# Attention quads from the sixth on: another order of VectorE's work, a Newton step moved to GpSimd, output tiles joined, weight pieces moved

## The chip, the cores and the metric

The kernel runs on one core of a Trainium2 chip. A core has five engines that each take their own queue of instructions in order: TensorE (matrix products, PE in the profile, with its weight loads as PEld), VectorE (DVE), ScalarE (ACT), GpSimd (POOL) and SyncE (SP, which here only issues DMA transfers). Engines wait for each other through semaphores. The metric is the device time of one execution in microseconds; the time before is the median of three runs, 825.98 us (824.99 to 826.01).

## The reference

An attention block with normalised q and k feeds a block with a SoLU activation. Shapes: 8 batches, 12 heads, 448 positions, head size 64; 3584 tokens, 768 features, 1024 hidden columns. All in fp32.

```python
q_n = q / sqrt(mean(q*q, -1) + 1e-6) * g_q        # k_n likewise
scores = q_n @ k_n.T / sqrt(64)
attn = exp(scores - max) / (sum(exp(scores - max)) + 1e-9)
x = (attn @ v) laid out as tokens x (heads * 64)  # 3584 x 768
h = x @ w_in                                      # 768 x 1024
solu = h * softmax(h)
ln = (solu - mean) / sqrt(var + 1e-6) * g_ln
out = ln @ w_out                                  # 1024 x 768
```

The weights w_in and w_out come as 64-bit floats and are turned into fp32 in the kernel.

## The kernel before

`fast_path` has three stages: attention (0 to 332.7 us of the profile), the product with w_in and the activation (to about 585 us), and the product with w_out (to the end). The order of the work in each engine's queue is the order in which the Python code emits it, by hand; `later(x, f)` puts f off until x further units of TensorE work have been emitted.

**Attention.** Two heads of one batch are a pair; there are 48. Two pairs are a quad; the loop over `m` runs over 24 quads, and in quad m the pairs are `a = 2m` and `b = 2m + 1`. One quad's work on TensorE: `scores(a, 0..2)` (keys against queries, 128 of the 448 keys in each), `scores_last` (the last 64 keys of both pairs in one tile), `scores(b, 0..2)`, then `values_last` and `values` for both pairs (exponentials times v, into PSUM tiles `o`), then `sums` (exponentials times a matrix of ones, which gives the softmax's denominators). ScalarE takes the exponential of each score tile (L802) into `E`. There is no subtraction of the maximum: q and k are normalised, so the scores are bounded.

To save TensorE work in `sums`, VectorE adds tiles first. `add(n)` makes `es` from E of key blocks 0 and 1 (L839). In the last two quads (`on_vector`, L833) `add_more` adds block 2 as well (L844). In all other quads block 2 is a term of its own in `sums` (L884): five terms instead of three, each of four products.

`inverse(m)` reads the sums from PSUM (a transpose on VectorE, L895, then a reciprocal, L896), and GpSimd copies 32x14 pieces of `rc` across partitions (L903, four copies). `divide(m)`, one unit later, spreads `rc` with a transpose (L910) and multiplies the tile `o` by it (L911), for each of the two pairs. `store_x` sends the result `xo` to DRAM on SyncE's queue.

**Normalisation of q and k for the next quads.** `load(n)` issues eight DMAs of 56 KB for one pair into a tile `qk` (five buffers). `squares` (ScalarE, L656), `row_sums` (VectorE, L664), `fold_sums` (GpSimd, four copies L674 and an addition L675), `rsqrt_seed` (ScalarE, logarithm and exponential, L694 and L695), `rsqrt_step` (a Newton step of four small VectorE instructions, L701 to L704), `normalise` (GpSimd, L713, 128x896, 1.70 us), `qk_transpose` (VectorE, L723) and `gain` (ScalarE, L727) make `qkT` for the scores. In quads 4 to 22 of before, seed, step and both `normalise` stand at the head of a quad, the transposes near its middle, and the squares, row sums and fold for the quad after it at its end.

**w_in under the attention.** Twelve pieces of w_in (512 KB each) are loaded (`load_next`), converted in two steps on ScalarE (L535, L536) and two on VectorE (`join`, L541, L542), and combined on GpSimd (`combine_in`, L563, 1.28 us), since the two later products use a seven-multiplication scheme that needs differences of blocks. `steps_at` and `joins_at` say in which quad. In most quads `load_v`, `store_x`, the loads of the pairs of quad m + 3 and a piece of w_in follow each other on SyncE's queue.

**The first product.** `in_parts` runs over 14 groups of two token tiles; the products use PSUM banks A, B, C, D. After a tile's last product, `done` emits `ff_max` and then `ff_exp`, `ff_mult`, `ff_moments`, `ff_norm` (ScalarE, L1077) and `ff_spread` (a VectorE transpose and four DMAs), each put off by so many units. The last of these, for the last group, come among the first products with w_out, where ScalarE must copy partial results out of PSUM (L1206) and copy operands (L1149, L1151, L1153).

Of the kernel before, what the change touches and what calls it, by code (L numbers as in the profile page):

```python
# [9 lines left out]
FP32 = mybir.dt.float32  # L10
# [356 lines left out]
def fast_path(  # L367
# [329 lines left out]
    def rsqrt_step(d):  # L697
# [5 lines left out]
        nc.vector.tensor_tensor(x, x, y, OP.mult)  # L703
        nc.vector.scalar_tensor_tensor(y, x, 1.5, y, OP.add, OP.mult)  # L704

    def normalise(n, e=nc.gpsimd):
        d = st[n]
        if ("one", n) in norms:
            y = norms["one", n]["y"]
        else:  # L710
            y = norms[n // 2]["y"][:, n % 2 * 2 * NB : (n % 2 + 1) * 2 * NB]
        d["qkn"] = work.tile([P, 2 * NB, 32], FP32, tag="qkn", name="qkn", bufs=2)
        e.tensor_tensor(  # L713
            d["qkn"],
            d["qk"].rearrange("p s b d -> p (s b) d"),
            y.rearrange("p b -> p b ()").to_broadcast([P, 2 * NB, 32]),
            OP.mult,
        )
# [41 lines left out]
    def warm_up():  # L760

        w = work.tile([P, 2, S], FP32, tag="r", name="warm", bufs=1)[:, 0]
        nc.vector.memset(w, 0.0)
        o = ps_t.tile([P, S], FP32, tag="o", name="pt", bufs=2)
        for _ in range(5):
            nc.tensor.matmul(o, w[:, 0:P], w, start=True, stop=True)

# [5 lines left out]

    def transpose_rows(n, s):
        d = st[n]
        d["pt", s] = ps_t.tile([P, S], FP32, tag="o", name="pt", bufs=2)
# [53 lines left out]

    def on_vector(m):  # L833
        return m >= NQ - 2

    def add(n):
        d = st[n]
# [2 lines left out]

    def add_more(n):
        d = st[n]
        if on_vector(n // 2):
# [26 lines left out]
    def sums(m):  # L870


        d = quads[m]
        sm = d["sm"] = ps_t.tile([P, S // 2], FP32, tag="t", name="sm")
        terms = [(2, d["E", NJ])]
        for key in ("es",) if on_vector(m) else (2, "es"):
            for i in range(2):
                n = st[2 * m + i]
                terms.append((i, n["E", 2] if key == 2 else n["es"]))
        for x, (w, e) in enumerate(terms):  # L880
            for h in range(2):
                for t in range(2):
                    g = 32 * (2 * h + t)
                    nc.tensor.matmul(  # L884
                        sm[g : g + 32, :], ones[:, w], e[:, h, t * S // 2 : (t + 1) * S // 2],
                        start=(x == 0), stop=(x == len(terms) - 1),
                    )
# [15 lines left out]
                nc.gpsimd.tensor_copy(rc[o : o + 32, :, t], rc[a : a + 32, :, t])  # L903

    def divide(m):
        xo = quads[m]["xo"] = work.tile([P, 2, S], FP32, tag="xo", name="xo", bufs=1)
        for i in range(2):
            n = 2 * m + i
            r = work.tile([P, NB, 32], FP32, tag="r", name="r", bufs=1)
            nc.vector.transpose(r, quads[m]["rc"][:, i].rearrange("p t b -> p (t b) ()").to_broadcast([P, NB, 32]))  # L910
            nc.vector.tensor_tensor(xo[:, i], st[n]["o"], r.rearrange("d b i -> d (b i)"), OP.mult)  # L911
            del st[n]

    def store_x(m):
        b, hp = divmod(2 * m, NP)
# [52 lines left out]
    def products(g, done):  # L968
# [5 lines left out]
        def mul(bank, a, i, begin=True):  # L974
            a11, a12, a21, a22 = gs[g, "A"]
            sm = gs[g, "s"]
            a = {"a11": a11, "a12": a12, "s3": a21, "a22": a22, "s1": sm[:, 0], "s2": sm[:, 1], "s4": sm[:, 2]}[a]
            if begin:
                tag = "t" if bank in "AC" or bank == "B" and g == NG - 1 else "o"
                k[bank] = ps_t.tile([P, 512], FP32, tag=tag, name=bank, bufs=3 if tag == "t" else 2)[:, 0:n]  # L980
# [373 lines left out]
    with tc.manual_schedule():  # L1354
# [19 lines left out]
        for m in range(NQ):  # L1374
# [7 lines left out]
            next1 = m + 1 < NQ  # L1382
            next2 = m + 2 < NQ
            next3 = m + 3 < NQ
            if m == 0:
                unit(lambda: scores(a, 0))
                normalise_rows(1, 0)
# [326 lines left out]
```

## Time and profile before

| | us |
|---|---|
| median of three runs | 825.98 |
| the profiled execution | 827.41 |
| its span | 825.1 |
| attention, to the first product with w_in | 332.7 |
| quad 6 to quad 23, starts of the scores | 96.66 to 320.53 |
| TensorE busy | 802.1 |
| VectorE busy | 617.7 |
| ScalarE busy | 474.6 |
| GpSimd busy | 468.5 |

A line of the profile's groups gives source line, engine, operation, tiles (out<-in), shape and count, busy time and mean ns of one, and then the idle time in front with what ended it. A line of a timeline gives start and length in us, engine, line, operation, tiles, shape, count, and in brackets the idle time before it and its releaser. A line of stretches gives the stretch, its length, the busy time of each engine with the number of instructions, the granted TensorE clock (1.00 is full), the share of the DMA engines and GB/s.

### The profile page before, as it was taken

Reading aid. Unit: us, or ns where it says so; the run is one execution under the profiler, and the core shown is the slowest. Engines: PE = TensorE matmul, PEld = TensorE weight load, DVE = VectorE, ACT = ScalarE, POOL = GpSimd, SP = SyncE. Lnnn points to the kernel's source line nnn. Section 1 sums busy time; section 2 is a strip of 40 time slices with the busy share of each in tenths; the row PEclk is TensorE's granted clock in tenths of the full one; section 3 lists DMA queues with packets and bytes.
Section 4 is the critical chain, followed back from the end, with each engine's and each line's share of the span. In section 5 each row is a group of like instructions: output and inputs, shape, how many; then the busy total and the mean of one; then the engine's idle time right before and its main releaser. Section 6 shows DMA issues by size and latency. Waiting matters only on the chain.

```text
span 825.1 us, 14999 instructions
## 1 busy us (share of the span) xinstructions
PE 802.1 (97%) x5030; PEld 469.7 (57%) x5030; DVE 617.7 (75%) x1217; ACT 474.6 (58%) x785; POOL 468.5 (57%) x635
## 2 busy tenths in 40 slices
PE   8989999999999999999999999999799999999996
PEld 4333444333344443444444444444499999999996
DVE  6867889787888888378878766677776866866945
ACT  6676778676877777366666644444424464464420
POOL 1334545555555647333346467767387777877761
PEclk9999999999999999999999999999989999999999
DMA  7778677877777664235665335552547466475312
GB/s 132 146 140 195 145 177 162 186 150 173 156 176 169 134 158 120 84 104 133 180 163 152 92 97 133 135 143 67 153 128 244 141 219 213 137 248 195 131 58 82
DMA packets 272546, 122.74 MB, mean 149 GB/s; under 512 B 190540, under 2 KB 257612, under 8 KB 272460
## 3 DMA queue, kind: packets, MB, share of 16 engines
q1 hardware_dynamic: 257276, 111.79, 52.9%
q10 hardware_dynamic: 15184, 9.90, 4.4%
q8 instruction: 42, 0.69, 0.4%
q14 instruction: 44, 0.36, 0.1%
HBM read 84.94 MB, written 36.70 MB: 147 GB/s over the span
## 4 chain that ended last, share of the span: by engine, by line
PE 72%; SPq 6%; DVE 5%; DMA 4%; POOL 2%; issue 2%; ACT 2%; DVEq 0%; ACTq 0%; POOLq 0%
PE A L1194 15%; PE A L982 11%; PE B L1194 8%; PE o L865 7%; PE s L812 7%; PE B L982 7%; SPq L634 5%; PE C L982 4%; PE D L982 4%; PE C L1194 4%; PE sm L884 3%; DMA v<-in_v_dram 1%; PE s L825 1%; PE o L854 1%; DMA qk<-in_k_dram 1%
## 5 line engine op out<-in xcount | busy, mean ns | idle before, releaser
L802 ACT ACTIVATE E<-s 128x896 f32<-128x896 f32 x168 | 139.0, 935 | 14.3 <-PE s L812 14.1
L812 PE MATMUL s<-qkT 64*64 64x448 f32 x1152 | 121.3, 548 | 1.5 <-ACT E L802 0.9
L865 PE MATMUL o<-E,v 128*64 128x448 f32 x576 | 113.5, 543 | 0.0
L674 POOL COPY ss<-part 32x56 f32<-32x56 f32 x88 | 42.1, 478 | 99.2 <-DVE part L664 96.5
L713 POOL TENSOR_TENSOR qkn<-qk,ny 128x896 f32<-128x896 f32 x46 | 77.1, 1697 | 28.4 <-DMA qk<-in_k_dram 12.0
L1071 POOL TENSOR_TENSOR he<-he,mhalf 128x1 f32<-128x1 f32 x28 | 28.1, 1005 | 108.7 <-DVE he L1070 108.2
L812 PEld LDWEIGHTS s<-qkT 64*64 64x64 f32 x1152 | 47.3, 163 | 61.3 <-ACT E L802 31.6
L1194 PE MATMUL A<-w_out,sums 128*128 128x192 f32 x392 | 80.7, 329 | 1.1 <-ACT q L1206 0.7
L865 PEld LDWEIGHTS o<-E,v 128*64 128x64 f32 x576 | 39.2, 137 | 72.7 <-issue 64.0
L1194 PE MATMUL B<-w_out,sums 128*128 128x192 f32 x392 | 80.4, 328 | 0.0
L982 PE MATMUL B<-w_in,xsum 128*128 128x512 f32 x168 | 76.7, 593 | 0.6 <-POOL he L1071 0.6
L982 PE MATMUL A<-w_in,xg 128*128 128x512 f32 x168 | 74.7, 593 | 0.7 <-ACT u L989 0.7
L1053 ACT ACTIVATE u<-h,hmax 128x1024 f32<-128x1024 f32 x28 | 32.1, 1148 | 63.6 <-DVE hmax L1047 63.6
L1194 PEld LDWEIGHTS A<-w_out,sums 128*128 128x128 f32 x392 | 66.7, 191 | 2.2 <-issue 1.0
L1194 PEld LDWEIGHTS B<-w_out,sums 128*128 128x128 f32 x392 | 67.0, 192 | 0.1
L664 DVE TENSOR_REDUCE part<-sq 128x28 f32<-128x896 f32 x46 | 48.7, 1079 | 10.4 <-ACT sq L656 8.5
L982 PEld LDWEIGHTS B<-w_in,xsum 128*128 128x128 f32 x168 | 31.8, 190 | 41.1 <-issue 38.0
L982 PEld LDWEIGHTS A<-w_in,xg 128*128 128x128 f32 x168 | 31.8, 190 | 41.0 <-issue 39.1
L723 DVE STREAM_TRANSPOSE qkT<-qkn 128x896 f32<-128x896 f32 x46 | 49.0, 1093 | 6.6 <-POOL qkn L713 6.6
L839 DVE TENSOR_TENSOR es<-E 128x896 f32<-128x896 f32 x48 | 53.3, 1112 | 0.5 <-ACT E L802 0.5
L656 ACT ACTIVATE sq<-qk 128x896 f32<-128x896 f32 x46 | 43.5, 986 | 9.9 <-DMA qk<-in_k_dram 6.0
L1194 PE MATMUL A<-w_out,s 128*128 128x192 f32 x224 | 45.5, 326 | 0.0
(151 smaller groups left out, 1625.0 us busy)
## 6 DMA issues: line engine op xcount, KB each, us to landing
ur<-ud SPq DMA_DIRECT2D x60, 256.0 KB, 4.6
ud<-ub SPq DMA_DIRECT2D x112, 128.0 KB, 2.3
xd<-xo SPq DMA_DIRECT2D x24, 448.0 KB, 4.1
qk<-in_q_dram SPq DMA_DIRECT2D x184, 56.0 KB, 2.5
qk<-in_k_dram SPq DMA_DIRECT2D x184, 56.0 KB, 2.4
v<-in_v_dram SPq DMA_DIRECT2D x24, 384.0 KB, 4.2
out_dram<-P SPq DMA_DIRECT2D x19, 384.0 KB, 4.0
raw<-in_moe_w_in_dram SPq DMA_DIRECT2D x12, 512.0 KB, 5.1
```

What stands on the lines that cost most here:

```text
L634: nc.sync.dma_start(d["qk"][g * 32 : g * 32 + 32, s], src[b, h0 + g // 2].rearrange("(b t) (x d) -> x t b d", t=32, x=2)[g % 2],)
L656: nc.scalar.activation(d["sq"], d["qk"].rearrange("p s b d -> p (s b) d"), AF.Square)
L664: nc.vector.tensor_reduce(norms[m]["part"][:, i], st[n]["sq"], AX, OP.add)
L674: e.tensor_copy(ss[g * 32 : g * 32 + 32], part[o * 32 : o * 32 + 32])
L713: e.tensor_tensor(d["qkn"], d["qk"].rearrange("p s b d -> p (s b) d"), y.rearrange("p b -> p b ()").to_broadcast([P, 2 * NB, 32]), OP.mult,)
L723: nc.vector.transpose(d["qkT"].rearrange("p s t -> p (s t)"), d["qkn"].rearrange("p b d -> p (b d)"))
L802: nc.scalar.activation(d["E", kc], s[:, :, 0:S], AF.Exp)
L812: nc.tensor.matmul(s[c : c + D, h, 0:S], d["qkT"][hh, 1, keys], d["qkT"][hh, 0, :], start=True, stop=True,)
L839: nc.vector.tensor_tensor(d["es"], d["E", 0], d["E", 1], OP.add)
L865: nc.tensor.matmul(d["o"][h * D : (h + 1) * D, :], quads[n // 2]["v"][:, n % 2 * 2 + h, kc], d["E", kc][:, h], start=False, stop=(kc == NJ ...
L982: nc.tensor.matmul(k[bank], a[:, c], w_in[i][:, c], start=begin and c == 0, stop=c == HD - 1, skip_group_check=not begin,)
L1194: nc.tensor.matmul(k[bank], a[:, c].rearrange("p a i -> p (a i)"), w_out[:, area, i, c], start=begin and c == 0, stop=c == KC - 1, skip_gr ...
```

## The change

From quad 6 (`SETTLED`) on, a new branch of the loop emits the quad's work in another order:

- `load(a + 6)` comes before the first scores, ahead of `store_x`, and `load(b + 6)` behind it; `qk` has six buffers instead of five.
- `add_more` runs on VectorE for pair a of every quad from 6 on, and for both pairs from quad 21 on. The terms of `sums` follow that: four, then three.
- The seed stands behind `scores_last`; the Newton step is `rsqrt_step_apart`, five GpSimd instructions; both `normalise` follow it.
- The transposes of the next pairs stand behind `add(b)`; the row sums of pair a for the quad after the next at the quad's end, those of pair b at the head of the next quad, behind `inverse`, with `fold_sums`.
- The step `join` of a w_in piece stands between `add_more(a)` and `add(b)`.
- `steps_at` is 4 to 15, one piece in each quad; `joins_at` is one combination in each quad from 9 to 20.

In all quads, the two `o` tiles of a quad are one PSUM tile of two banks, and `divide` is one transpose and one product over both pairs. Banks B and D of the first product share that tile. The warm-up's and the first rows' tiles follow. For the last two groups of the first product the delays of the five steps are given one by one; those of the last group are longer.

```diff
-        d["qk"] = loads.tile([P, 2, NB, 32], FP32, tag="qk", name="qk", bufs=5)
+        d["qk"] = loads.tile([P, 2, NB, 32], FP32, tag="qk", name="qk", bufs=6)
...
+    def rsqrt_step_apart(d):
+
+        y, ss = d["y"], d["ss"]
+        p, w = ss.shape
+        x = small.tile([P, 4 * NB], FP32, tag="nx", name="nx", bufs=2)[0:p, 0:w]
+        nc.gpsimd.tensor_scalar(x, ss, -0.5 / D, -0.5e-6, OP.mult, OP.add)
+        nc.gpsimd.tensor_tensor(x, x, y, OP.mult)
+        nc.gpsimd.tensor_tensor(x, x, y, OP.mult)
+        nc.gpsimd.tensor_scalar(x, x, 1.5, 1.0, OP.add, OP.mult)
+        nc.gpsimd.tensor_tensor(y, x, y, OP.mult)
...
-    def on_vector(m):
-        return m >= NQ - 2
+    def on_vector(n):
+        m, i = divmod(n, 2)
+        return m >= NQ - 3 or m >= SETTLED and i == 0
...
     def values_last(m):
 
         d = quads[m]
+        o = d["o"] = ps_t.tile([P, 2, 512], FP32, tag="o", name="o", bufs=1)
         for i in range(2):
-            o = st[2 * m + i]["o"] = ps_t.tile([P, S], FP32, tag="o", name="o", bufs=2)
+            st[2 * m + i]["o"] = o[:, i, 0:S]
...
     def divide(m):
-        xo = quads[m]["xo"] = work.tile([P, 2, S], FP32, tag="xo", name="xo", bufs=1)
+        d = quads[m]
+        xo = d["xo"] = work.tile([P, 2, S], FP32, tag="xo", name="xo", bufs=1)
+        r = work.tile([P, 2 * NB, 32], FP32, tag="r", name="r", bufs=1)
+        nc.vector.transpose(
+            r, d["rc"].rearrange("p i t b -> p (i t b) ()").to_broadcast([P, 2 * NB, 32])
+        )
+        nc.vector.tensor_tensor(
+            xo, d["o"][:, :, 0:S], r.rearrange("d (i b) x -> d i (b x)", i=2), OP.mult
+        )
...
-            spread = {NG - 2: 7 - 2 * i, NG - 1: 8 - i}.get(g, 7)
-            for x, f in zip((1, 2, 3, 5, spread), (ff_exp, ff_mult, ff_moments, ff_norm, ff_spread)):
+            waits = {
+                (NG - 2, 1): (1, 2, 3, 5, 5), (NG - 1, 1): (1, 2, 3.25, 6.75, 7), (NG - 1, 0): (2.25, 3.75, 4.75, 7.5, 8)
+            }.get((g, i), (1, 2, 3, 5, 7))
+            for x, f in zip(waits, (ff_exp, ff_mult, ff_moments, ff_norm, ff_spread)):
...
-    steps_at = (4, 5, 6, 7, 8, 9, 10, 12, 14, 16, 18, 20)
-    joins_at = {9: (0,), 11: (1,), 13: (2,), 14: (3,), 15: (4,), 17: (5,), 19: (6,), 21: (7,), 22: (8, 9), 23: (10, 11)}
+    steps_at = tuple(range(4, 16))
+    joins_at = {9 + x: (x,) for x in range(12)}
+    SETTLED = 6
...
+            if m >= SETTLED:
+                for x in joins_at.get(m, ()):
+                    combine_in(x)
+                if next1:
+                    load_v(m + 1)
+                    if m > SETTLED:
+                        row_sums(b + 2)
+                        fold_sums(m + 1)
+                if next3:
+                    load(a + 6)
+                unit(lambda: scores(a, 0))
+                store_x(m - 1)
+                if next3:
+                    load(b + 6)
+                if m - 1 in sets:
+                    load_next()
+                unit(lambda: scores(a, 1))
+                unit(lambda: scores(a, 2))
+                unit(lambda: scores_last(m))
+                add(a)
+                if next1:
+                    rsqrt_seed(norms[m + 1])
+                    rsqrt_step_apart(norms[m + 1])
+                    normalise(a + 2)
+                    normalise(b + 2)
+                unit(lambda: scores(b, 0))
+                add_more(a)
+                step(m - 1)
+                unit(lambda: scores(b, 1))
+                add(b)
+                if next1:
+                    qk_transpose(a + 2)
+                unit(lambda: scores(b, 2))
+                add_more(b)
+                if next2:
+                    squares(a + 4)
+                if next1:
+                    gain(a + 2)
+                    qk_transpose(b + 2)
+                if next2:
+                    squares(b + 4)
+                if next1:
+                    gain(b + 2)
+                if next2:
+                    row_sums(a + 4)
+                begin(m)
+                unit(outputs)
+                unit(lambda: values(b))
...
+                unit(lambda: sums(m))
+                inverse(m)
+                if next1:
+                    later(1, lambda m=m: divide(m))
...
+                continue
```

More of the change, by code (lines that the diff above doesn't have):

```diff
@@ L763, in warm_up @@
         nc.vector.memset(w, 0.0)
-        o = ps_t.tile([P, S], FP32, tag="o", name="pt", bufs=2)
+        o = ps_t.tile([P, S], FP32, tag="t", name="pt")
         for _ in range(5):
@@ L775, in transpose_rows @@
         d = st[n]
-        d["pt", s] = ps_t.tile([P, S], FP32, tag="o", name="pt", bufs=2)
+        if s == 0:
+            d["pt"] = ps_t.tile([P, 2, 512], FP32, tag="t" if n else "o", name="pt", bufs=3 if n else 1)
+        d["pt", s] = d["pt"][:, s, 0:S]
         for j in range(4):
@@ L842, in add_more @@
         d = st[n]
-        if on_vector(n // 2):
+        if on_vector(n):
             nc.vector.tensor_tensor(d["es"], d["es"], d["E", 2], OP.add)
@@ L875, in sums @@
         terms = [(2, d["E", NJ])]
-        for key in ("es",) if on_vector(m) else (2, "es"):
+        for key in (2, "es"):
             for i in range(2):
-                n = st[2 * m + i]
-                terms.append((i, n["E", 2] if key == 2 else n["es"]))
+                n = 2 * m + i
+                if key == "es":
+                    terms.append((i, st[n]["es"]))
+                elif not on_vector(n):
+                    terms.append((i, st[n]["E", 2]))
         for x, (w, e) in enumerate(terms):
@@ L905, in divide @@
     def divide(m):
-        xo = quads[m]["xo"] = work.tile([P, 2, S], FP32, tag="xo", name="xo", bufs=1)
-        for i in range(2):
[L908 to L912, printed above, removed]
+        d = quads[m]
[7 more added lines that the diff above has]
+        )
+        for i in range(2):
+            del st[2 * m + i]
     def store_x(m):
@@ L978, in mul @@
             if begin:
-                tag = "t" if bank in "AC" or bank == "B" and g == NG - 1 else "o"
-                k[bank] = ps_t.tile([P, 512], FP32, tag=tag, name=bank, bufs=3 if tag == "t" else 2)[:, 0:n]
+                if bank in "AC" or bank == "B" and g == NG - 1:
+                    k[bank] = ps_t.tile([P, 512], FP32, tag="t", name=bank, bufs=3)[:, 0:n]
+                else:
+                    if "BD" not in k:
+                        k["BD"] = ps_t.tile([P, 2, 512], FP32, tag="o", name="BD", bufs=1)
+                    k[bank] = k["BD"][:, "BD".index(bank), 0:n]
             for c in range(HD):
@@ L1384, in fast_path @@
             next3 = m + 3 < NQ
+            if m >= SETTLED:
[46 more added lines that the diff above has]
+                unit(lambda: values(b))
+                if m == NQ - 1:
+                    block_sums(0, 0)
+                    block_sums(0, 1)
+                    load_x(1)
+                unit(lambda: sums(m))
+                inverse(m)
+                if next1:
+                    later(1, lambda m=m: divide(m))
+                if m == NQ - 2:
+                    load_x(0)
+                    sizes(0)
+                continue
             if m == 0:
```

## The prediction

> **What bounds the kernel now.** I read the page, then the stretches, the waits, and the timelines of single engines. The page gives a span of 825.1 us, 827.41 us for the profiled execution; the three runs have a median of 825.98 us. I work in differences and add them to the median.
>
> ```profile
> PE 802.1 (97%) x5030; PEld 469.7 (57%) x5030; DVE 617.7 (75%) x1217; ACT 474.6 (58%) x785; POOL 468.5 (57%) x635
> PE 72%; SPq 6%; DVE 5%; DMA 4%; POOL 2%; issue 2%; ACT 2%; DVEq 0%; ACTq 0%; POOLq 0%
> ```
>
> TensorE is the bound on average, but SyncE's queue holds 6% of the chain. Quad 17 and quad 13, by stretch (length, then PE, PEld, DVE, ACT, POOL busy):
>
> ```profile
> 251.50:264.40 12.90, 12.90 (x130) 5.44 (x128) 11.39 (x19) 9.14 (x14) 6.87 (x11) 1.00 0.73 160
> 199.90:212.80 12.90, 10.84 (x116) 4.22 (x118) 10.98 (x18) 9.68 (x14) 8.12 (x12) 1.00 0.75 159
> ```
>
> The first is a full quad of matmuls, 12.90 us. In the second TensorE loses 2.06 us. There SyncE is late: the square of q and k waits 3.3 us for its DMA, the sums on VectorE follow, and TensorE waits 1.5 us for `es`. SyncE issues the v load of quad 7 at 99.53 and of quad 22 at 300.28: 13.38 us a quad over 15 quads, nearly back to back, while its waits for engines there come to some 5 us. So the loads nearly pace quads 6 to 20. By the starts of L812, quad 6 begins at 96.66 and quad 23 at 320.53: 223.87 us for 17 quads, 13.17 each.
>
> Now VectorE against GpSimd. The sum `es` (L839), the fold's copies (L674), min/median/max in ns, and two pieces of timeline:
>
> ```profile
> L839 DVE TENSOR_TENSOR es<-E x48: 1046/1080/2161, 14.6 to 326.6; 128x896 f32<-128x896 f32 x48
> L674 POOL COPY ss<-part x88: 219/227/952, 29.3 to 307.7; 32x56 f32<-32x56 f32 x88
> 22.89 1.70 POOL L713 TENSOR_TENSOR qkn<-qk,ny 128x896 f32<-128x896 f32 x1 [2.16 <-DVE ny L704]
> 23.76 1.78 DVE L839 TENSOR_TENSOR es<-E 128x896 f32<-128x896 f32 x1
> ```
>
> The addition at 23.76 ends 0.95 us after GpSimd's product: it waited for it. A 0.22 us copy takes 0.95 us when an addition is under way, and ends just behind it. One excludes the other. Transposes, reductions and the products with PSUM next to L713 stretch neither side. Quads of before keep the additions away from the long products.
>
> Last, the start of the second product:
>
> ```profile
> 595.61 1.24 ACT L1077 ACTIVATE u<-u,shift,he 128x1024 f32<-128x1024 f32 x1 [4.19 <-POOL shift L1073]
> 597.63 1.65 PE L1194 MATMUL A<-w_out,a 128*128 128x192 f32 x4 [3.83 <-ACT u L1206]
> ```
>
> ScalarE's queue stands behind L1077, TensorE waits 3.83 us, and then four matmuls take 1.5 us instead of 0.81: the granted clock is half until 602.9.
>
> **What the Trainium skill says.** "GPSIMD Engine Reference", Specifications: GpSimd shares its SBUF interfaces with VectorE, and contends with VectorE instructions that have two SBUF inputs. The trace agrees (1.08 to 2.16 us for L839). "TensorE: Matmul & The Clock Gate", Part 1: an idle window of about 3.4 us halves the clock. The 3.83 us wait agrees.
>
> **The change, part by part.** *Ones products.* A term is eight records of L884; the group takes 2.03 us with five terms and 1.27 with three, so 0.38 us a term. Quads 6 to 20 lose one, quad 21 two: 17 x 0.38 = 6.5 us of TensorE. A quad would be 12.52 us.
>
> *Third additions.* One more L844 in those quads, 1.08 us alone, up to 1.89 against GpSimd. VectorE gives back Newton (0.13 + 0.24 + 0.22 + 0.22 = 0.81) and in `divide` four instructions become two: 2 x 644 + 2 x 624 = 2.54 becomes 1.09 (as L723, 896 wide) + 1.09 (624 plus 448 columns at the slope of L839 against L1208, 1.08 - 0.35 over 704) = 2.18. It is about even, with 11.4 us busy of 12.9 in a quad with a join.
>
> *Newton on GpSimd.* Five 128x56 instructions. The nearest row is L675, 302 ns, and 0.08 us of gap behind its producer. The bounds are 0.2 us (the copies) and 0.45 with gap; I take 0.38, 1.9 us.
>
> *The new order, where it costs.* `row_sums(b+2)` goes behind `inverse`, and `fold_sums`, seed, Newton and both `normalise` all fall into the same quad, ahead of `qk_transpose(b+2)` and `row_sums(a+4)`, which stand before the next `inverse` on VectorE. That closes a loop. Quads 9 to 16 (join and combine), t from the start of `inverse`:
> - VectorE: inverse 0.42 + 0.33; row sums end at 1.8. GpSimd: four rc copies (0.88) end at 1.83, combine (1.28) at 3.15, four fold copies (0.26 each) at 4.3.
> - VectorE: divide 1.9 to 4.1, then `add(a)` to 5.2. The fold's addition comes just behind its start and ends at 5.35.
> - ScalarE: seeds (0.34 + 0.25) to 6.1, and only then E(b,0) and E(b,1) (0.80 apart, 0.97 each), at 7.9.
> - VectorE has `add_more` (1.0) and the two join instructions (0.72, 0.69) to 7.6, and `add(b)`, which needs E(b,1), to 9.1. One Newton step passes at the end of each: 7.1, 7.8, 8.2, 9.25, 9.65.
> - GpSimd: L713 twice, 1.65 + 1.70, to 13.0. VectorE: second transpose (1.05) 14.1, row sums (1.0) 15.1: the next inverse.
>
> So some 15.0 us against TensorE's 12.52. Behind VectorE's wait for `qkn` stand the row sums, the next inverse and divide; behind ScalarE's wait for the fold stand the exponentials of b; TensorE waits for both, at `scores_last` for `gain(b+2)` and for the bank that the inverse frees. Quads 17 to 20 have no join: Newton ends at 8.05, the product stands behind `add(b)` until 8.95, and the loop is 14.3. Quads 7 and 8 have no combine: 14.6. Quad 6 starts in step: 13. Quad 21 (both third additions) 14.6, quad 22 (no row sums ahead) 14.3. Sum: 13 + 2 x 14.6 + 8 x 15.0 + 4 x 14.3 + 14.6 + 14.3 = 248.3. Against 223.9 that is +24.4 us. These quads also hide SyncE's 13.38.
>
> *Loads.* The sixth buffer and eight DMAs of `load(a+6)` ahead of `store_x` let SyncE run ahead; `xd` now stands behind them, about 4.4 us later (eight issues at 0.48 plus gaps), and `divide` waits for it through the single `xo`. Bytes are the same; raw pieces come in quads 5 to 14 on end, combines from quad 9 to 20. Hidden while the loop is slower than SyncE; if the loop is short, this is the next bound.
>
> *PSUM.* One two-bank tile instead of two: `values_last` waits for the whole divide, 4.1 us into a quad, and starts at 5.3. Nothing. With B and D in one tile, B waits for the same read by VectorE as before. Nothing; at most 0.7 us (L998) in each of 13 groups if D waits for B.
>
> *Times in the last group.* L1077 leaves the place ahead of the copies: 3.83 us, half of the 5.3 us at half clock (2.6) and the 0.72 us wait at 589.66 can go, 7.2 in all. But the copies of a22 (L1153) stand in the same queue and need a `ur` transfer that lands at 596.82, so part of the wait moves there. Between 0 and 7.2 I take 5.
>
> The sum: 825.98 + 24.4 - 5 = 845.4, forecast 845.
>
> **Rivals.** *The loop stays shorter than the queue of loads (faster).* If Newton and the fold slip between VectorE's instructions, the same chain without any exclusion is 1.83 + 1.3 + 1.4 + 0.7 + 1.9 + 3.4 + 2.1 = 12.6 us, TensorE's 12.52 almost. Then SyncE's 13.38 stays the bound for quads 6 to 20 and little is gained there, 0 to 8 us if the new order saves its waits; with the 5 us, 813 to 821, say 818. It decides at a mean of (223.9 + 5) / 17 = 13.46 us a quad: below that the change is faster. For it: the row sums, transposes and rc copies do not contend. Against: L674 was held in all 17 quads in which it met L839.
>
> *The loop binds, but milder.* Newton at 0.2 us a step, the first product ahead of `add(b)`: 13.5 to 14 us a quad, 17 x 13.75 = 233.8, +9.9 - 5: 831.
>
> *TensorE's idle time halves its clock.* 2.5 us idle a quad is in pieces under 2 us, so this is unlikely; if it comes in some quads, over 858.
>
> **How the numbers follow.** Loop as worked out, 832 to 858: 0.52. Milder, 826 to 832: 0.16. Fast, 812 to 822: 0.25. Half clock: 0.07. The range of 814 to 858 leaves out the last and a little of the fast case; the likeliest case alone has 834 to 857. About 0.2% (1.7 us) is what a measurement can tell from no change. Faster 0.26, same 0.03, slower 0.71.
>
> **What would show it.** After, L884 should fall to 32 records a quad from quad 6. The loop shows as starts of L895 14 to 15 us apart in quads 9 to 16, in step with the starts of L812, VectorE waiting for `qkn` ahead of its transposes, Newton steps on GpSimd of 0.3 to 1.0 us, and additions over 1.5 us where L713 runs. The loads show as SyncE waiting for engines. At the start of the second product, the 3.83 us wait and the half clock should be gone. I am wrong if quads 9 to 16 start 13 us apart or less, or if the additions stay at 1.08 us beside L713.

## The result and the profile after

The changed kernel takes 854.21 us (median of 4 runs, 853.59 to 856.0) where the kernel before takes 826.00 on the same chip (824.99 to 826.04). The ratio is 1.0355, 95% interval 1.0323 to 1.0387: 28 us slower. The forecast was 845. The profiled execution below is the slowest of the four, 856.0 us.

The page of the changed kernel, its busy times and its chain of work:

```profile
PE 806.5 (94%) x4894; PEld 459.5 (54%) x4894; DVE 623.5 (73%) x1118; ACT 476.6 (56%) x785; POOL 518.4 (61%) x720
PE 56%; DVE 12%; SPq 9%; POOL 7%; DMA 7%; issue 5%; ACT 3%; POOLq 0%; DVEq 0%; ACTq 0%
```

TensorE's share of the chain fell from 72% to 56%; VectorE, GpSimd and ScalarE grew from 9% to 22% together. GpSimd is busy 50 us longer and VectorE 6 us, although the work taken from VectorE and the work given to it are about even.

The starts of the `inverse` transposes (L895 before, L913 after) and of the first and last matmuls of the two products cut the two profiled executions into pieces:

| piece | before, us | after, us | difference | forecast |
|---|---|---|---|---|
| to the inverse of quad 0 | 26.49 | 30.09 | +3.60 | 0 |
| inverse of quad 0 to that of quad 5 | 70.31 | 69.26 | -1.05 | 0 |
| inverse of quad 5 to that of quad 22 | 223.87 | 250.65 | +26.78 | +24.4 |
| inverse of quad 22 to that of quad 23 | 12.14 | 13.61 | +1.47 | 0 |
| to the start of the first product's last matmul | 253.59 | 253.54 | -0.05 | 0 |
| from there to the first matmul with w_out | 0.43 | 1.44 | +1.01 | -5 with the next |
| products with w_out | 232.23 | 229.56 | -2.67 | |
| end of the last matmul to the end of the span | 6.09 | 6.45 | +0.36 | 0 |
| span | 825.1 | 854.6 | +29.5 | +19.4 |

**The loop.** In quads 9 to 16, which have a join, the inverses now start 15.13 to 15.15 us apart, in quads 17 to 20, which have none, 14.93 or 14.94, in quads 6 to 8 14.06 or 14.07. One stretch from inverse to inverse of the changed kernel without a join, then one with (length; PE, PEld, DVE, ACT, POOL busy; granted clock; DMA share; GB/s):

```profile
277.61:292.55 14.94, 13.18 (x120) 4.89 (x120) 11.62 (x13) 9.37 (x14) 10.63 (x17) 1.00 0.60 125
217.25:232.40 15.15, 13.28 (x120) 4.80 (x120) 11.67 (x15) 10.54 (x16) 11.17 (x17) 1.00 0.70 157
```

No engine is full; TensorE idles 1.8 us a quad. Now the rows of the first addition and of the fold's copies, min/median/max in ns, and the timelines of GpSimd and VectorE within the first of these stretches, the one without a join:

```profile
L853 DVE TENSOR_TENSOR es<-E x48: 1049/1082/2628, 18.2 to 357.5; 128x896 f32<-128x896 f32 x48
L674 POOL COPY ss<-part x88: 221/226/1142, 32.9 to 339.5; 32x56 f32<-32x56 f32 x88
```

```profile
281.36 1.40 POOL L674 COPY ss<-part 32x56 f32<-32x56 f32 x2
282.84 1.19 POOL L675 TENSOR_TENSOR ss<-ss,part 128x56 f32<-128x56 f32 x1
284.12 0.24 POOL L711 TENSOR_SCALAR nx<-ss 128x56 f32<-128x56 f32 x1
...
285.93 0.31 POOL L715 TENSOR_TENSOR ny<-nx,ny 128x56 f32<-128x56 f32 x1
286.31 4.20 POOL L724 TENSOR_TENSOR qkn<-qk,ny 128x896 f32<-128x896 f32 x2
```

```profile
281.59 1.08 DVE L853 TENSOR_TENSOR es<-E 128x896 f32<-128x896 f32 x1
282.77 1.09 DVE L858 TENSOR_TENSOR es<-es,E 128x896 f32<-128x896 f32 x1
286.33 2.62 DVE L853 TENSOR_TENSOR es<-E 128x896 f32<-128x896 f32 x1 [2.47 <-ACT E L815]
288.88 1.10 DVE L734 STREAM_TRANSPOSE qkT<-qkn 128x896 f32<-128x896 f32 x1
290.55 1.11 DVE L734 STREAM_TRANSPOSE qkT<-qkn 128x896 f32<-128x896 f32 x1 [0.57 <-POOL qkn L724]
291.58 1.04 DVE L664 TENSOR_REDUCE part<-sq 128x28 f32<-128x896 f32 x1
292.55 0.40 DVE L913 STREAM_TRANSPOSE r<-sm 128x224 f32<-128x224 f32 x1
```

Read them against each other. The last fold copy ends with the addition at 281.59, not before it. The fold's addition (L675) ends only behind the third addition at 282.77, 1.19 us for work of 0.30. ScalarE's seed waits for it, and with the seed the exponentials of pair b, so VectorE stands idle for 2.47 us. Then the second `add` starts 0.02 us behind GpSimd's first product and takes 2.62 us, and the second product stands behind that addition: 4.20 us for two that take 3.35 alone. The two transposes, the row sums and the next inverse follow as a row. In a quad with a join the last meeting falls the other way round:

```profile
226.28 4.08 POOL L724 TENSOR_TENSOR qkn<-qk,ny 128x896 f32<-128x896 f32 x2
225.97 1.18 DVE L853 TENSOR_TENSOR es<-E 128x896 f32<-128x896 f32 x1 [1.03 <-ACT E L815]
```

There the second `add` starts first, and the first product stands behind it. That is the loop of the prediction, though some of its meetings fall elsewhere, as told below.

**The start.** First lines of TensorE in the kernel before, then TensorE and ScalarE in the changed one:

```profile
10.61 2.52 PE L812 MATMUL s<-qkT 64*64 64x448 f32 x24 [0.62 <-ACT qkT L786]
13.06 0.98 PE L778 MATMUL pt<-ident,x 112*128 112x112 f32 x8
```

```profile
8.77 1.21 PE L791 MATMUL pt<-ident,x 112*128 112x112 f32 x8 [1.23 <-DVE x L783]
11.18 4.21 PE L825 MATMUL s<-qkT 64*64 64x448 f32 x24 [1.21 <-ACT qkT L799]
15.33 0.60 PE L791 MATMUL pt<-ident,x 112*128 112x112 f32 x4
16.96 0.60 PE L791 MATMUL pt<-ident,x 112*128 112x112 f32 x4 [1.03 <-ACT qkT L797]
...
10.07 0.63 ACT L797 ACTIVATE qkT<-pt,gcol 128x448 f32<-128x448 f32 x1 [1.27 <-PE pt L791]
```

The transposed first rows of q and k now share one PSUM tile. ScalarE's read of q starts at 10.07 instead of 9.47, behind the transposes of k; TensorE waits 1.21 us instead of 0.62, and its 24 score products take 4.21 us instead of 2.52. The granted clock is half from 11.8 to 15.2 us. The transposes of pair 1's k then wait another 1.03 us for the read of its q, which is in the same tile. The first inverse is 3.6 us late.

**The start of the second product.** ScalarE and TensorE of the changed kernel:

```profile
626.93 1.24 ACT L1103 ACTIVATE u<-u,shift,he 128x1024 f32<-128x1024 f32 x1 [1.22 <-POOL shift L1099]
629.22 0.62 ACT L1177 COPY a<-ur 128x512 f32<-128x512 f32 x1 [1.05 <-DMA ur<-ud]
```

```profile
630.11 0.92 PE L1222 MATMUL A<-w_out,s 128*128 128x192 f32 x4 [0.54 <-ACT u L1234]
632.36 1.06 PE L1222 MATMUL B<-w_out,sums 128*128 128x192 f32 x4 [1.33 <-DVE P L1284]
633.22 1.49 PE L1222 MATMUL C<-w_out,a 128*128 128x192 f32 x4
634.50 1.49 PE L1222 MATMUL A<-w_out,sums 128*128 128x192 f32 x4
```

The single wait of 3.83 us is gone. Waits of 0.54 and 1.33 us stand a few groups later, and one of 0.67 us for GpSimd's sums at 645.5. ScalarE waits there for a transfer; VectorE's last read of bank B (L1284, at 632.00) stands behind a transpose of 1.23 us (L1112, at 630.84). The half clock comes all the same, at 633.0 to 636.4.

### The profile page after: what moved, and what is told of

It reads as the page before. It is cut to its first block, busy times and chain, and to the rows that moved or that the text cites. A ratio compares the mean times of both kernels' runs of the same rounds, so it can differ in the third digit from the quotient of the medians.

```text
span 854.6 us, 14661 instructions
## 1 busy us (share of the span) xinstructions
PE 806.5 (94%) x4894; PEld 459.5 (54%) x4894; DVE 623.5 (73%) x1118; ACT 476.6 (56%) x785; POOL 518.4 (61%) x720
## 4 chain that ended last, share of the span: by engine, by line
PE 56%; DVE 12%; SPq 9%; POOL 7%; DMA 7%; issue 5%; ACT 3%; POOLq 0%; DVEq 0%; ACTq 0%
PE A L1222 14%; PE BD L1008 10%; PE A L1008 10%; SPq L634 7%; PE B L1222 7%; PE C L1008 4%; POOL qkn L724 4%; PE C L1222 3%; DMA qk<-in_k_dram 3%; PE s L825 3%; PE o L880 2%; DVE qkT L734 2%; DVE part L664 2%; DVE xo L930 1%; ACT E L815 1%
## 5 line engine op out<-in xcount | busy, mean ns | idle before, releaser
L815 ACT ACTIVATE E<-s 128x896 f32<-128x896 f32 x168 | 141.0, 915 | 12.4 <-PE s L825 10.2
L825 PE MATMUL s<-qkT 64*64 64x448 f32 x1152 | 128.7, 564 | 19.8 <-ACT qkT L738 10.8
L724 POOL TENSOR_TENSOR qkn<-qk,ny 128x896 f32<-128x896 f32 x46 | 88.6, 1945 | 29.4 <-DVE ny L704 20.5
L825 PEld LDWEIGHTS s<-qkT 64*64 64x64 f32 x1152 | 44.9, 165 | 89.8 <-ACT E L815 32.8
L853 DVE TENSOR_TENSOR es<-E 128x896 f32<-128x896 f32 x48 | 61.2, 1275 | 18.3 <-ACT E L815 18.3
L1008 PE MATMUL BD<-w_in,xsum 128*128 128x512 f32 x156 | 71.2, 592 | 0.0
L738 ACT ACTIVATE qkT<-qkT,gcol 128x448 f32<-128x448 f32 x46 | 30.7, 673 | 59.5 <-DVE qkT L734 57.9
L921 POOL COPY rc<-rc 32x14 f32<-32x14 f32 x96 | 18.4, 191 | 65.2 <-DVE rc L914 60.4
L674 POOL COPY ss<-part 32x56 f32<-32x56 f32 x88 | 32.3, 367 | 28.9 <-DVE part L664 25.2
L1008 PEld LDWEIGHTS BD<-w_in,xsum 128*128 128x128 f32 x156 | 29.5, 190 | 37.5 <-issue 35.2
```

The costliest lines, as they stand in the source:

```text
L674: e.tensor_copy(ss[g * 32 : g * 32 + 32], part[o * 32 : o * 32 + 32])
L724: e.tensor_tensor(d["qkn"], d["qk"].rearrange("p s b d -> p (s b) d"), y.rearrange("p b -> p b ()").to_broadcast([P, 2 * NB, 32]), OP.mult,)
L815: nc.scalar.activation(d["E", kc], s[:, :, 0:S], AF.Exp)
L825: nc.tensor.matmul(s[c : c + D, h, 0:S], d["qkT"][hh, 1, keys], d["qkT"][hh, 0, :], start=True, stop=True,)
L853: nc.vector.tensor_tensor(d["es"], d["E", 0], d["E", 1], OP.add)
L1008: nc.tensor.matmul(k[bank], a[:, c], w_in[i][:, c], start=begin and c == 0, stop=c == HD - 1, skip_group_check=not begin,)
```

## The experiments

Theory: the new order closes a loop through VectorE, GpSimd and ScalarE, and the loop is long because GpSimd's instructions and VectorE's instructions with two SBUF inputs exclude one another. Rivals: the added third additions and joined tiles cost by themselves; VectorE's time is the cause and not the exclusion; the loads set the pace. Attention times below run from the inverse of quad 5 to that of quad 23: 236.01 us before, 264.26 after. The kernel before had medians of 823.87 to 824.32 us in these runs; a ratio is always to the kernel before on the same chip.

**The old order with the other parts kept.**

```diff
-            if m >= SETTLED:
+            if m >= NQ:
                 for x in joins_at.get(m, ()):
```

> The changed kernel with quads 6 on in the old order: Newton on VectorE, normalise at the top of the quad, fold two quads ahead. Third additions of pair a, the joined output tile, the w_in pieces, the sixth buffer and the new times in the last group stay. Theory (the new order closes a loop through VectorE, GpSimd and ScalarE): the starts of the inverse in quads 6 to 20 fall from 14.1-15.1 us apart to 12.9-13.4, and the time from 854.2 to about 827, 822 to 832. Rival (the third additions and the joined tiles cost by themselves, whatever the order): above 843.

Measured: 823.13 us, ratio 0.9994 (0.9982 to 1.0006); attention 234.49 us, quads mostly 13.12 apart with joins and 12.78 without. The edit sends all quads through the old branch, so the Newton step is on VectorE again and the loads stand at their old places on SyncE's queue. The new branch as a whole is worth 264.26 - 234.49 = 29.8 us, more than the whole loss. The rest of the change is about neutral. One stretch of this kernel, from inverse to inverse:

```profile
190.67:203.79 13.12, 13.03 (x124) 4.78 (x120) 12.07 (x19) 10.34 (x15) 8.87 (x13) 1.00 0.82 183
```

VectorE is busy 12.07 of 13.12 us here, and 11.67 of 15.15 in the changed kernel: the slower order is the one with the emptier VectorE.

**The additions with one input.**

```diff
-        nc.vector.tensor_tensor(d["es"], d["E", 0], d["E", 1], OP.add)
+        if SETTLED <= n // 2 < NQ - 3:
+            nc.vector.transpose(d["es"].rearrange("p h t -> p (h t)"), d["E", 1].rearrange("p h t -> p (h t)"))
+        else:
+            nc.vector.tensor_tensor(d["es"], d["E", 0], d["E", 1], OP.add)
```

`add_more` is changed in the same way, with block 2.

> The changed kernel with the additions of es in quads 6 to 20 (first and third ones, both pairs) put as transposes of the same 128x896 on VectorE, which have one input in SBUF and take the same 1.1 us; the sums over keys are left out by that, nothing else. Theory (an addition and a GpSimd instruction exclude one another, and that lengthens the loop): the fourth fold copy falls from 1.13 to 0.22 us, the fold's addition from 1.19 to 0.3, the products stay at 1.7; quads 9 to 20 fall to 13.0 to 13.5 us; 829, 825 to 836. Rival (it is VectorE's own time and order that make the loop, not the exclusion): within 1 us a quad of the changed kernel, 842 to 855.

Its whole time, 2373.55 us, says nothing: without the sums the kernel goes on to its general path, which does all the work a second time and whose lines fill the trace from 819 us on. Ahead of that it can be read. Quads 9 to 16 start 13.20 or 13.21 us apart, quads 17 to 20 12.26 to 12.52. Stretches, then GpSimd and VectorE of one quad:

```profile
189.52:202.73 13.21, 12.95 (x124) 4.89 (x120) 11.41 (x15) 10.56 (x16) 8.91 (x17) 1.00 0.79 174
254.61:266.87 12.26, 12.26 (x124) 5.11 (x120) 10.23 (x12) 9.37 (x13) 7.96 (x17) 1.00 0.74 152
```

```profile
270.07 1.02 POOL L674 COPY ss<-part 32x56 f32<-32x56 f32 x4
271.17 0.30 POOL L675 TENSOR_TENSOR ss<-ss,part 128x56 f32<-128x56 f32 x1
...
273.75 3.35 POOL L724 TENSOR_TENSOR qkn<-qk,ny 128x896 f32<-128x896 f32 x2
```

```profile
270.84 1.10 DVE L854 STREAM_TRANSPOSE es<-E 128x896 f32<-128x896 f32 x1
272.04 1.11 DVE L862 STREAM_TRANSPOSE es<-E 128x896 f32<-128x896 f32 x1
273.77 1.11 DVE L854 STREAM_TRANSPOSE es<-E 128x896 f32<-128x896 f32 x1 [0.62 <-ACT E L815]
```

VectorE's instructions take the same 1.1 us, stand in the same places and order, and wait for the same producers. They are transposes now and have one SBUF input, and every stretched time of this quad is gone: L675 is 0.30 us although a VectorE instruction runs beside it from 270.84 to 271.94, the two products 3.35, the VectorE instruction beside them 1.11. That it is the second input and not the kind of instruction is seen in the changed kernel: the product in `divide` (L930, 220.22 to 221.31) has one input in PSUM, and three of GpSimd's copies beside it take 0.76 us together, 0.22 or 0.23 each. The loop is 1.9 to 2.7 us shorter. So the exclusion is what makes the loop long, which settles the second rival. And quads of 12.26 us with their loads of q, k and v in them speak against the rival that the loads set a pace of 13.4.

**Without the third additions of pair a.**

```diff
-        return m >= NQ - 3 or m >= SETTLED and i == 0
+        return m >= NQ - 3
```

> The changed kernel without the third additions of pair a in quads 6 to 20: VectorE has 1.09 us less a quad, TensorE one ones term, 0.38 us, more. Theory (loop): this addition stands between the last fold copy and the fold's addition and ahead of the join, so about 0.9 us leaves the loop: 14.2 us a quad in 9 to 16, 14.0 in 17 to 20; 841, 837 to 846. If TensorE's work set the time: 15 x 0.38 more, 860. If the third additions were the whole cause: 826 to 832.

Measured: 843.06 us, ratio 1.0232 (1.0189 to 1.0275); quads 9 to 16 mostly 14.37, quads 17 to 20 14.05, attention 252.64. The third additions cost the changed kernel 11.6 us of its attention: 0.77 us in a quad of 9 to 16 and 0.88 in one of 17 to 20, less than their own 1.09, and the loop without them is still over 14, so they are not the whole cause. TensorE's added 0.38 us a quad is not seen.

**The Newton step back on VectorE.**

```diff
-                    rsqrt_step_apart(norms[m + 1])
+                    rsqrt_step(norms[m + 1])
```

> The changed kernel with the Newton step back on VectorE (four instructions, at the place where GpSimd's five are issued, between the additions of pair a). Theory (loop with exclusion): the step itself ends some 1.5 us earlier, but the third addition and the two join instructions now stand behind it, beside GpSimd's products, and push them and the transposes back: quads 17 to 20 14.4, quads 9 to 16 15 to 17; 858, 850 to 868. Rival (GpSimd's slower step is the cause): 1.5 us a quad less, 832 to 838.

Measured: 861.69 us, ratio 1.0442 (1.0407 to 1.0477); quads 9 to 16 16.04, quads 17 to 20 14.02. In quads 17 to 20 the step ends 6.9 us behind the inverse instead of 8.6, half of it because the fold's addition no longer meets the third one (0.30 us instead of 1.19), and the quad gains 0.9; where the two join instructions stand behind it they meet the products and take 2.19 and 2.07 us instead of 0.7, and the quad loses 0.9. On balance, moving Newton to GpSimd was by itself a gain in this order.

**The fold ahead of the inverse.**

```diff
-                    if m > SETTLED:
-                        row_sums(b + 2)
-                        fold_sums(m + 1)
...
                     row_sums(a + 4)
+                    row_sums(b + 4)
+                    fold_sums(m + 2)
                 begin(m)
```

> The changed kernel with one move: the row sums of b and the fold for quad m+2 stand at the end of quad m, ahead of the inverse, and no more behind the inverse of quad m+1 in the quad that uses them. Every instruction stays. Theory (loop): the seed no longer waits for what follows the inverse; Newton and the products start some 1.5 to 2 us earlier, but row sums of 1.0 us come ahead of the inverse: 13.6 to 14.1 us a quad in place of 15.1 and 14.9; 839, 832 to 845. Rival (VectorE's added work, or the loads, set the pace): 15 us a quad stays, 853 to 856.

Measured: 865.30 us, ratio 1.0500 (1.0456 to 1.0544); quads 9 to 16 15.46 to 16.35, quads 17 to 20 14.47 to 14.55. Neither expectation held: 11 us slower than the changed kernel, with no instruction added. GpSimd and VectorE in a quad of 16.35 us:

```profile
215.12 0.95 POOL L714 TENSOR_SCALAR nx<-nx 128x56 f32<-128x56 f32 x1
216.16 1.18 POOL L715 TENSOR_TENSOR ny<-nx,ny 128x56 f32<-128x56 f32 x1
217.42 2.03 POOL L724 TENSOR_TENSOR qkn<-qk,ny 128x896 f32<-128x896 f32 x1
```

```profile
217.09 0.79 DVE L541 SCALAR_TENSOR_TENSOR tmp<-raw,tmp 128x512 uint32<-128x512 uint32 x1
217.92 2.07 DVE L542 SCALAR_TENSOR_TENSOR w_in<-raw,tmp 128x512 uint32<-128x512 uint32 x1
219.91 2.58 DVE L853 TENSOR_TENSOR es<-E 128x896 f32<-128x896 f32 x1
222.42 1.10 DVE L734 STREAM_TRANSPOSE qkT<-qkn 128x896 f32<-128x896 f32 x1
```

The step and the products did come earlier, as meant. But earlier put the last Newton steps into the additions of pair a, and the products into the second join instruction and the addition of pair b, which are in front of the transposes in VectorE's queue. Counted from the inverse, the products end at 11.5 us instead of 13.1, but the transposes begin at 12.4 instead of 11.5, and the row sums of pair b, 1.0 us, now also come ahead of the next inverse. The dependency was cut, and the shared access took its place.

**Both together.** The fold ahead of the inverse, and the additions with one input.

> The kernel with the fold ahead of the inverse, with the additions of es in quads 6 to 20 put as transposes of one input (sums left out, and what depends on them after the attention takes another way; only the attention is read). Theory (the earlier Newton steps gained little because they ran into the additions): quads 17 to 20 fall from 14.5 to 12.5 us, 12.2 to 12.9, quads 9 to 16 from 15.9 to 13.2, 12.9 to 13.6. Rival (the row sums ahead of the inverse and the rc copies behind the fold are what cost): 14 us and more, 15 us in 9 to 16.

Here too only the attention is read. Quads 17 to 20: 12.31 to 12.78 us, as the theory has it. Quads 9 to 16: 15.13 to 15.42, the rival's figure but not its reason, since the row sums and copies that it blames are in quads 17 to 20 too. The trace of the second kind shows what differs: the two join instructions still have two SBUF inputs, take 1.16 (1.45 in one quad) and 2.07 us beside the products, and hold `add(b)`, both transposes and two row sums behind them. So the theory has to be told with its meetings: it isn't enough to count additions, every two-input instruction that falls beside GpSimd's products counts.

**The first rows in two tiles.**

```diff
-            d["pt"] = ps_t.tile([P, 2, 512], FP32, tag="t" if n else "o", name="pt", bufs=3 if n else 1)
-        d["pt", s] = d["pt"][:, s, 0:S]
+        pt = ps_t.tile([P, 2, 512], FP32, tag="t" if s else "o", name="pt", bufs=3 if s else 1)
+        d["pt", s] = pt[:, 0, 0:S]
```

> The changed kernel with the transposed first rows in two PSUM tiles again (queries and keys apart), nothing else. Theory (the joined tile makes ScalarE's read of the first half wait for the transposes of the second, TensorE idles 0.6 us longer and its clock is halved for 3.4 us): the first inverse starts near 26.5 us in place of 30.1, no half clock before 30 us, and some 2.5 us of it last to the end: 851.7, 850.5 to 853. Rival (the 3.6 us are caught up by quad 6 and hidden by the loop): 853.5 to 855.

Measured: 851.69 us, ratio 1.0326 (1.0297 to 1.0355), where the changed kernel has 1.0355. First inverse at 26.28 us, no half clock, and the inverse of quad 5 at 95.87 instead of 99.35: 3.5 us, all of which last to the end of the matmuls. The step ahead of the products with w_out fell too, from 1.44 to 0.43 us, though nothing was changed there. The edit shifts by one which of the three buffers of that PSUM tag comes next; that this is the reason was not tried. The products themselves take 229.51 us, and the half clock among them is missing in this profile. By the two intervals alone the gain is not certain, and the two profiles are of the slowest execution there and the fastest here; what they show is where the time at the start went.

**The new times of the last group alone, on the kernel before.**

```diff
-            spread = {NG - 2: 7 - 2 * i, NG - 1: 8 - i}.get(g, 7)
-            for x, f in zip((1, 2, 3, 5, spread), ...
+            waits = {
+                (NG - 2, 1): (1, 2, 3, 5, 5), (NG - 1, 1): (1, 2, 3.25, 6.75, 7), (NG - 1, 0): (2.25, 3.75, 4.75, 7.5, 8)
+            }.get((g, i), (1, 2, 3, 5, 7))
```

> The kernel before with only the new times of the last group of the first product. Theory (the blocked place in ScalarE's queue goes, a wait for a transfer and a short half clock stay; the 0.85 us wait of the joined bank is not there): 2.7 to 3.6 us faster, 822.9, 822 to 824. By the prediction's term of 5: 821. Rival (the stall only moves on to the transfer): 825.5 to 826.5.

Measured: 822.90 us, ratio 0.9979 (0.9964 to 0.9994). By the profile the products with w_out take 229.52 us instead of 232.23, the 2.7 us of the changed kernel, but without any half clock there. The measured ratio is worth 1.7 us, 0.5 to 3.0.

**Two kernels put together from the parts that helped.** The first has the changed kernel's parts with the old order, without the third additions of pair a, and with the first rows in two tiles:

> The changed kernel with the old order of the quads, without the third additions of pair a in quads 6 to 20, and with the first rows in two PSUM tiles; joined output tile, w_in pieces, sixth buffer and new times stay. Theory (in the old order the third addition fills VectorE to 13.1 us a quad and so gives TensorE's saving away): quads 6 to 20 at TensorE's 12.9 us, 231 to 233 us from the inverse of quad 5 to that of 23, the start 2 us earlier: 818.8, 817 to 821. Rival (the queue of loads holds quads at 13.1 to 13.4 anyway): 235 us for the attention's quads, 821.5 to 824.

Measured: 821.96 us (818.5 to 825.0), ratio 0.9950 (0.9925 to 0.9975): faster than both kernels, and the largest gain of these runs. Its profiled execution was the slowest of nine, 825.01 us, with 237.04 us of attention: in quads 14 to 16, 13.9 to 14.2 us apart, ScalarE waits up to 1.9 us for q and k from DRAM. In that execution the rival held, and the median is the rival's as well. Four of the nine executions took 818.5 to 819.9 us, the theory's time; none of these was profiled. The time of the third additions in the old order can't be read from it.

The second is the kernel before with the new times, the w_in pieces one per quad and the sixth buffer:

> The kernel before with the new times of the last group, the w_in pieces one per quad (conversion in quads 4 to 15, one combination in each of quads 9 to 20) and a sixth buffer for q and k; order, additions and PSUM tiles as before. Theory (the slow quads 14.5 and 15.2 of before are late loads, which the sixth buffer and the even pieces mend): all quads at 12.9 to 13.0, 231 to 233 us from the inverse of quad 5 to that of 23 in place of 236; 818.5, 816.5 to 821. Rival (a combine and a join in every quad from 9 to 16 slow them as much as the loads did): 822 to 824.

Measured: 822.28 us (817.7 to 827.2), ratio 0.9984 (0.9964 to 1.0003). In its profiled execution, 819.92 us, all quads from 6 to 21 but one take 12.89 or 12.90 us and the attention 231.01. ScalarE's waits from 96 to 310 us, in the kernel before and then in this one (total, times, longest):

```profile
ACT sq L656 <- DMA qk<-in_k_dram: 5.1, 3, 3.3
ACT sq L656 <- DMA vl<-in_v_dram: 2.6, 1, 2.6
```

```profile
ACT sq L656 <- DMA qk<-in_k_dram: 1.3, 2, 1.0
```

In this execution a combine in each of quads 9 to 20, with a join up to quad 16, costs nothing in the old order. But over 22 runs the times spread by 9 us, ten of them at 817.7 to 821.1 and the others up to 827.2, and the interval of the ratio includes 1, that is no gain. Late loads that come back in some executions are the likely reason; no slow one was profiled.

## Why the prediction was right or wrong

**Loop of quads 9 to 16: right.** 15.0 us was worked out, 15.13 to 15.15 measured. The first three Newton steps end 7.1, 7.8 and 8.2 us behind the inverse, as worked out, and the second product at 13.1 instead of 13.0. In between two errors cancel, which is luck: the fold's addition ends 1.07 us later than the prediction has it (6.42 against 5.35), so `add(b)` ends at 9.9 instead of 9.1; but it starts too late to hold a Newton step, the last of which ends at 8.96 instead of 9.65, and the first product then waits for `add(b)`. The additions with one input show that the mechanism is right: the prediction has 12.6 us for the chain without any exclusion, and quads 17 to 20 took 12.26 to 12.52 without it.

**Loop of quads 17 to 20: right in kind, 0.63 us short each.** The step "the fold's addition comes just behind its start and ends at 5.35" failed. It ends 6.4 us behind the inverse: the last copy waits for the first addition, and then the fold's addition waits for the third one, since GpSimd's next instruction is ready just after VectorE has begun its next. And the first product doesn't stand behind `add(b)`: `add(b)` starts 0.02 us behind it, and the second product stands behind that.

**Quads 6 to 8, 21, 22.** Forecast 13.0, 14.6, 14.6, 14.6, 14.3; measured 14.06, 14.07, 14.06, 14.41, 13.17. "Quad 6 starts in step" was wrong, as was quad 22 kept near the full loop. The sum over quads 6 to 22 was 248.3 against 250.65, off by 2.35. In quads 21 and 22 TensorE waited 1.76 and 1.50 us for `es` of the third addition (L858). Quad 23 wasn't in the sum. Its `scores_last` waits for an exponential:

```profile
352.47 5.74 ACT L815 ACTIVATE E<-s 128x896 f32<-128x896 f32 x7
353.42 0.98 PE L838 MATMUL s<-qkT 64*64 64x448 f32 x8 [1.29 <-ACT E L815]
```

The last transpose now ends just behind the inverse of quad 22, so ScalarE's `gain` comes at 350.10, the sums for the first product (L965) at 350.68 to 352.57, and only then the exponentials, 2.5 us behind the inverse; with the old order it was 1.0. That is the +1.47 us.

**"PSUM. ... Nothing": wrong at the start.** This is the largest miss of a term put at nothing. The prediction looked at `o`, B and D, which are indeed free: the first product takes as long as before. It passed over the tiles of the first rows, which are put into the same two-bank shape. There, one tile makes each reader wait for the writer of the other half; 3.6 us were lost at the first inverse, 2.0 of them without the half clock too (28.45 in the old order against 26.49). Up to quad 5 1.05 us was won back, probably by the joined `divide`, which is on the path of the first quads and was not tried alone.

**"Times in the last group ... between 0 and 7.2 I take 5": mis-sized.** The wait and its half clock were the two terms. Part of the wait moved on to the transfer, as the prediction said (0.54 us), more of it to bank B and to GpSimd's sums (1.33 and 0.67), and a half clock of 3.4 us stayed. From the last matmul with w_in on, the step and the products took 231.00 us instead of 232.66: 1.66 won, 1.3 with the other small differences. With the same times but no half clock there, the runs of the old order, of the new times alone, of the first rows in two tiles and without the third additions took 229.9 to 230.0, that is 2.7 won. So the half clock is 1.0 us of what is missing, and the waits that came instead are the other 2.3. The 1.01 us more ahead of the first product, at a bank that VectorE still read, are not a loss in that sum: the old order has them as well.

**Third additions "about even" and Newton at 0.38 us.** The Newton instructions take 0.24 to 0.31 us where nothing meets them, 0.56 and more where an addition does. VectorE's total was right, and beside the point: the third addition costs 0.8 us a quad in this order, in which it meets the fold's addition. Without it that addition takes 0.62 us instead of 1.19 in a quad with a join.

**The loads "nearly pace quads 6 to 20": wrong.** 13.38 us was SyncE's pace in a kernel in which the quads themselves took 13.17. The kernel before with the sixth buffer issued the same loads in 12.90 us a quad in its profiled execution.

Added up against the span: +2.35 (size of the loop), +1.47 (quad 23), +2.55 (start), +3.7 (last group), that is 10.1 of the 29.5 - 19.4 us.

## What to carry to other kernels

Work that is handed to GpSimd is free only while VectorE runs instructions that don't take its SBUF access: list, for each GpSimd instruction, which two-input VectorE instruction will be in flight when it comes up, and what waits for each of them. When a step is moved to start earlier, look at what it now meets: a dependency that is cut can come back as a meeting on the shared access, and make the kernel slower. When several tiles are joined in one shape, follow every user of that shape, the start-up code first, because there nothing hides a wait.

## What the runs showed of the hardware that was not expected

The exclusion depends on the second SBUF input and not on how long VectorE is busy: transposes of 1.10 us left a GpSimd addition at 0.30 us and two products at 3.35, where additions of 1.08 us made it 1.19 and 4.20; and a product with one input in PSUM left three copies at 0.22 or 0.23 us. The Trainium skill has this in "SBUF — State Buffer", "SBUF: two separate sides": the shared pair of ports is an exclusive lock, held for a whole instruction, and who comes first gets it. The trace agrees in both directions: `add(b)` behind a product, 2.62 us, and a product behind `add(b)`, 4.20 for two. The prediction had read the pieces of it from the trace; what it had not worked out is how much depends on who comes first by 0.02 or 0.07 us.

In these profiles TensorE's clock at the start hangs on tenths of a microsecond. With the same code up to quad 5, the first inverse came at 30.0 to 30.2 us in the changed kernel and four of the experiments, with a half clock from between 11.2 and 11.8 us on, and at 28.45 in the two others with the joined rows (the old order, and the one-input additions), with full clock and 2.52 us for the first scores. In those two, the wait ahead of the first transposes was 0.98 and 0.74 us long instead of 1.23, since the product in front of it came 0.2 to 0.4 us later. The Trainium skill, "TensorE: Matmul & The Clock Gate", Part 1, says that the window in which activity is counted runs freely, so that the same kernel can come out either way; two outcomes 1.6 us apart at the first inverse, from the same code up to there, agree with that. But no idle window of about 3.4 us, which the prediction took from the same part, stands ahead of these half clocks: two waits of 1.23 and 1.21 us with transposes between them were enough at the start, and at the second product 0.54 and 1.33 us led to half clock while a single wait of 2.15 or 2.16 us (old order, no third additions) did not. In the kernel before it set in at 596.1 us, 2.3 us into the wait of 3.83. What rule fits all of these stays open.
